# Two small numbers checked on VectorE instead of in every engine's registers, in an attention-and-mixer kernel on one core

## The chip, the core and the metric

The kernel runs on one core of a Trainium2 chip. A core has five engines that each work through a queue of their own: PE (TensorE, matmuls, with PEld for its weight loads), DVE (VectorE), ACT (ScalarE), POOL (GpSimd) and SP (SyncE, which here only issues DMAs). The metric is the device time of one execution in microseconds (us), lower is better.

## The reference, cut to what matters

Four sequences of 768 positions, 8 heads of 64 channels. Attention is banded: a query sees the first `n_global` keys (8 here) and the last `n_local` keys up to itself (96 here), with a linear distance bias. Its output goes through a token-mixing and a channel-mixing network.

```python
is_global = pos[None, :] < int(n_global)
is_local = (rel >= 0) & (rel < int(n_local))
keep = is_global | is_local
...
scores = scores - np.max(scores, axis=-1, keepdims=True)
a = np.exp(scores)
a = a / (np.sum(a, axis=-1, keepdims=True) + 1e-09)
return np.matmul(a, v).astype(np.float32)
...
h = np.maximum(xt @ w_tok1, 0.0) @ w_tok2
u = x + h.transpose(0, 2, 1)
h2 = np.maximum(u @ w_ch1, 0.0) @ w_ch2
return (u + h2).astype(np.float32)
```

## The kernel before

`n_global` and `n_local` are inputs, 64-bit integers that arrive as four 32-bit words `n`. The kernel holds two programs: `fast`, for `n_global` from 0 to 32 and `n_local` from 1 to 97, and `dense` for all else. Every engine reads the four words from DRAM into registers (first the pointer, `n_ptr`, then `n`), joins six comparisons in `near` with register instructions, and branches. The inputs here take `fast`.

`Early` is issued ahead of the branch. It starts the DMAs of the keys and queries of the first three units into ring slots `e0`, `e1` and `e3` (in the profile all are `e`, in order rows `e_58`, `e_59` and `e_61`; `e_60` is slot 2, a scratch area), the DMA of the two numbers into `ni` (all 128 partitions), and lets POOL prepare index patterns (`rel`, `far`, `glob`) and the table of powers `sc`. `warm` issues four dummy matmuls of 512 columns.

Behind the branch, `Fast.setup` scales query 0 on DVE (`scale`, result in `qs`), turns the numbers into three columns `few`, and builds the bias tiles `bo`, `bt` (DVE) and `be` (POOL) and the identity `ident` (POOL).

Then a planner (`Plan`) sets all further order. A work item has a rank, costs and dependences; `record` replays them in a model and issues them engine by engine. `InOrder` pins the order of one engine's instructions. The ranks come from a packed table `RANKS`, one number for each item. Items of a *unit* v (256 queries of a pair of heads; 48 units, 12 a batch): `load`, `q` (scale the query, mostly on POOL), `S` (scores `sp` on PE), `max` (DVE adds the bias and takes the maximum, into `pp` or `p`), `exp` (ACT), `sum`, `inv`, `norm`, transposes `tp` or DMA transposes by way of `r`, `V` (PE, into `op`), and `put` (into `x`, the attention's output; in batch 0 ACT copies the reciprocal factors, then DVE multiplies). Middle units (j = 1) span the border of two halves of `x`, so their `put` is two copies of 128 columns and two products. Weights come as 64-bit floats and are decoded by ACT and DVE (`w`, `t`). The mixers' matmuls are `pj`, `pu`, `hp` and `acc`; the last batch's channel mixer uses products `X`, `Y`, `W`, `ga` and `ge`.

## Time and profile before

| | |
|---|---|
| Median of three runs | 600.99 us (600.99 to 601.85) |
| The profiled execution: its time | 601.2 us |
| its span, first to last instruction | 599.1 us |
| PE, DVE, ACT, POOL busy | 587.3, 392.8, 297.3, 177.6 us |
| DMA | 64.22 MB, mean 107 GB/s |

The span is 2.1 us shorter than the execution's time; what lies outside it is not in the profile. Times in all views count from the span's start. Matmuls are pipelined and their ends are modelled, so PE's busy time overlaps and is no proof of a full rate; the distance from start to start tells more. A wait on several semaphores is put down to the one that came last by the profile. A `q` behind an engine's name stands for its sequencer, which loads registers, branches and issues DMAs.

### The profile page before, as it was taken

What the parts mean: (1) busy time and instruction counts of PE and PEld (TensorE: products, weight loads), DVE (VectorE), ACT (ScalarE), POOL (GpSimd) and SP (SyncE); (2) the same over time, 40 slices, a digit from 0 to 9 for tenths busy, and PEclk for the clock granted to TensorE, in tenths of its full rate; (3) what the DMA queues carried; (4) which work ended last, traced back from release to release, by engine and by line L of the source; (5) the groups of instructions that cost most, each with busy time, mean ns of one, the idle gap of its engine ahead of it and who ended that gap; (6) DMA issues with size and microseconds to landing.
All of it is one profiled execution on the core that took longest, in us unless ns stands there. A gap on an engine that the chain in (4) does not pass through costs nothing.

```text
span 599.1 us, 10678 instructions
## 1 busy us (share of the span) xinstructions
PE 587.3 (98%) x3804; PEld 537.7 (90%) x3804; DVE 392.8 (66%) x1026; ACT 297.3 (50%) x778; POOL 177.6 (30%) x265
## 2 busy tenths in 40 slices
PE   7999999999999999999999999999999999999996
PEld 4878898899899999999898999999889999999995
DVE  5999889999542475356666475555877569764323
ACT  5999988876521244255543135473543244232310
POOL 3345695664320054033242134243330020000000
PEclk9999999999999999999999999999999999999999
DMA  6981273576541014736736411657535001000003
GB/s 238 408 305 37 93 278 147 162 170 120 141 101 40 14 40 54 184 78 144 176 72 133 95 54 29 149 141 160 158 72 110 14 2 40 14 1 0 1 2 110
DMA packets 90717, 64.22 MB, mean 107 GB/s; under 512 B 76192, under 2 KB 80672, under 8 KB 90656
## 3 DMA queue, kind: packets, MB, share of 16 engines
q1 hardware_dynamic: 90512, 63.46, 39.4%
q8 instruction: 32, 0.52, 0.4%
q14 instruction: 29, 0.24, 0.1%
q10 hardware_dynamic: 144, 0.00, 0.0%
HBM read 38.80 MB, written 6.29 MB: 75 GB/s over the span
## 4 chain that ended last, share of the span: by engine, by line
PE 56%; DMA 3%; DVE 2%; issue 0%; ACT 0%; SPq 0%; DVEq 0%
PE acc L63 16%; PE hp L63 13%; PE ga L63 6%; PE X L63 4%; PE op L63 3%; PE pj L63 3%; PE pu L63 3%; PE ge L63 3%; PE sp L63 2%; PE W L63 2%; DMA p<-r 2%; PE Y L63 1%; DMA xn<-xr 1%; DVE r L63 1%; DVE o L63 1%; DVE p L63 0%
## 5 line engine op out<-in xcount | busy, mean ns | idle before, releaser
L63 PE MATMUL hp<-uh,wc 128*128 128x384 f32 x576 | 153.9, 336 | 0.2 <-DVE hl L63 0.2
L63 PE MATMUL acc<-hh,wc 128*128 128x384 f32 x576 | 149.0, 339 | 0.9 <-DVE st L63 0.9
L63 PEld LDWEIGHTS acc<-hh,wc 128*128 128x128 f32 x576 | 102.8, 188 | 7.4 <-issue 4.3
L63 PEld LDWEIGHTS hp<-uh,wc 128*128 128x128 f32 x576 | 104.6, 188 | 3.1 <-issue 1.7
L63 POOL TENSOR_SCALAR p<-p,st 128x256 f32<-128x256 f32 (+1 forms) x132 | 77.8, 607 | 78.1 <-ACT p L63 40.7
L63 PE MATMUL acc<-hl,wc 128*128 128x384 f32 x288 | 96.6, 335 | 0.1
L63 PE MATMUL hp<-ul,wc 128*128 128x384 f32 x288 | 96.3, 334 | 0.0
L63 DVE COPY r<-p 128x1024 uint16<-128x1024 uint16 (+1 forms) x89 | 63.7, 732 | 40.3 <-DMA p<-r 24.9
L63 ACT ACTIVATE hh<-hp 128x384 fp32r<-128x384 f32 x72 | 35.0, 488 | 83.2 <-PE hp L63 50.4
L63 ACT ACTIVATE p<-p,st 128x256 f32<-128x256 f32 (+1 forms) x132 | 63.5, 484 | 14.4 <-DVE st L63 13.8
L63 DVE SCALAR_TENSOR_TENSOR hl<-hp,hh 128x384 fp32r<-128x384 f32 x72 | 39.5, 551 | 33.6 <-ACT hh L63 32.0
L63 PEld LDWEIGHTS acc<-hl,wc 128*128 128x128 f32 x288 | 54.1, 188 | 0.4 <-DVE hl L63 0.4
L63 PEld LDWEIGHTS hp<-ul,wc 128*128 128x128 f32 x288 | 54.1, 188 | 0.2
L63 POOL TENSOR_TENSOR ul<-x,uh 128x384 fp32r<-128x384 f32 x23 | 25.4, 1109 | 94.3 <-ACT uh L63 92.4
L63 POOL TENSOR_SCALAR qs<-e,sc 128x256 f32<-128x256 f32 x36 | 22.7, 630 | 77.1 <-DMA e<-pk 59.1
L63 ACT COPY r<-p 128x1024 uint16<-128x1024 uint16 (+1 forms) x23 | 29.1, 1285 | 29.1 <-DMA p<-r 17.5
L63 PE MATMUL sp<-e,qs 64*128 64x256 f32 (+1 forms) x312 | 39.3, 389 | 3.0 <-DVE e L63 3.0
L63 PEld LDWEIGHTS sp<-e,qs 64*128 64x128 f32 x312 | 27.8, 197 | 10.9 <-issue 8.4
L63 ACT COPY x<-op 128x256 f32<-128x256 f32 (+1 forms) x64 | 18.9, 322 | 25.6 <-PE op L63 25.4
L63 PE MATMUL ga<-hh,wc 128*128 128x512 f32 x96 | 30.2, 395 | 0.0
L63 ACT ACTIVATE pp<-pp,st 128x256 f32<-128x256 f32 (+1 forms) x60 | 28.5, 483 | 1.9 <-DVE st L63 1.9
L63 DVE CUSTOM_DVE_ANT_0 p<-sp,be 128x256 f32<-128x256 f32 x48 | 20.0, 416 | 12.2 <-PE sp L63 10.8
(146 smaller groups left out, 1105.2 us busy)
## 6 DMA issues: line engine op xcount, KB each, us to landing
w<-wc SPq DMA_DIRECT2D x24, 512.0 KB, 5.4
e<-pk SPq DMA_DIRECT2D x24, 512.0 KB, 4.0
e<-pk SPq DMA_DIRECT2D x12, 384.0 KB, 3.9
out<-o SPq DMA_DIRECT2D x24, 192.0 KB, 1.9
unit<-pk SPq DMA_DIRECT2D x7, 512.0 KB, 8.7
w<-w SPq DMA_DIRECT2D x6, 512.0 KB, 9.5
out<-x SPq DMA_DIRECT2D x8, 192.0 KB, 2.1
p<-r SPq DMA_TRANSPOSE x56, 3.2
```

The costliest lines, as they stand in the source:

```text
L63: ins = getattr(self.engine, name)(*args, **kw)
```

## The change

The engines no longer load `n`. ACT's DMA brings the four words into one partition; DVE makes them floats (`num`), and tests all four ranges at once: (word - middle)² - (half width)² is at most 0 where a word is in range, and the maximum of the four is the `flag`. Every engine loads that one word from SBUF and branches on it. A matmul with a row of ones (`wide`) copies the numbers to all partitions. It stands between two groups of four dummy matmuls, where there was one group. The bias tiles `bo` and `bt` and the identity are built ahead of the branch. Queries are scaled in place, without `qs` and its three buffers and tokens; query 0 is scaled on ACT. `put` of middle units in batch 0 becomes one copy and one product of 256 columns. The planner starts from other busy times, and the table of ranks is new; of it only the first line of each is shown.

```diff
 FIRST = 0
-WARM = 4
+WARM = 4, 4
...
     def __getattr__(self, name):
         def call(*args, **kw):
             ins = getattr(self.engine, name)(*args, **kw)
-            if self.last is not None:
-                self.tc.add_manual_dep(ins.ins, self.last.ins.name, mybir.DependencyInfo(
-                    mybir.DependencyClass.NoSync, mybir.DependencyReason.DATA), reason="order")
-            self.last = ins
+            self.follow(ins)
             return ins
         return call
 
+    def follow(self, ins):
+        if self.last is not None:
+            self.tc.add_manual_dep(ins.ins, self.last.ins.name, mybir.DependencyInfo(
+                mybir.DependencyClass.NoSync, mybir.DependencyReason.DATA), reason="order")
+        self.last = ins
+
 
 class Early:
 
 
-    def __init__(self, tc, pool, pk, nb):
+    def __init__(self, ctx, tc, pool, pk, nb):
         nc = tc.nc
-        pe, dve, act, gps, sp = [InOrder(tc, e) for e in (nc.tensor, nc.vector, nc.scalar, nc.gpsimd, nc.sync)]
+        self.lines = pe, dve, act, gps, sp = [
+            InOrder(tc, e) for e in (nc.tensor, nc.vector, nc.scalar, nc.gpsimd, nc.sync)]
 
         self.slots = [pool.tile([P, 1024], F32, tag=f"e{i}", name=f"e{i}") for i in range(RING)]
-        self.ni = pool.tile([P, 4], I32, tag="ni", name="ni")
         self.ident = pool.tile([P, P], F32, tag="ident", name="ident")
         self.sc = pool.tile([P, H // 2], F32, tag="sc", name="sc")
-
+        self.bo, self.bt, self.be = [pool.tile([P, w], F32, tag=t, name=t) for t, w in (("bo", 256), ("bt", P), ("be", 256))]
+        bo = self.bo
+        ni = pool.tile([1, 4], I32, tag="ni", name="ni")
+        few = pool.tile([P, 32], F32, tag="first", name="first")
+        num, mid, far, n = few[0:1, 0:4], few[0:1, 4:8], few[0:1, 8:12], few[:, 20:23]
+        self.flag = few[0:1, 16:17]
+
+        act.dma_start(out=ni, in_=nb)
         t = self.slots[2]
-        self.zeros = t[:, 576:832].bitcast(BF16)
-        dve.memset(self.zeros, 0.0)
-
-        self.one = t[:, 832:836]
-        dve.memset(self.one, 0.0)
-        act.dma_start(out=self.ni, in_=nb.broadcast_to([P, 4]))
-        act.activation(out=self.one, in_=self.one, func=AF.Exp)
+        zeros, ones, one = t[:, 576:832].bitcast(BF16), t[0:1, 836:964], t[:, 832:836]
+        dve.memset(zeros, 0.0)
+        dve.memset(one, 0.0)
+        dve.memset(ones, 1.0)
+        for x, lo, hi in ((0, 0, 32), (1, 0, 0), (2, 1, 97), (3, 0, 0)):
+            gps.memset(mid[:, x:x + 1], (lo + hi) / 2)
+            gps.memset(far[:, x:x + 1], (hi - lo) ** 2 / 4)
+        act.activation(out=one, in_=one, func=AF.Exp)
         for i, x, k in ((0, 0, 128), (1, 1, 128), (2, 3, 0)):
             sp.dma_start(out=self.slots[x][:, k:640], in_=pk[i, :, k:640])
...
             gps.iota(t, pattern=[[step, t.shape[-1]]], base=base, channel_multiplier=mult,
                      allow_small_or_imprecise_dtypes=True)
 
-        self.rel, self.far, self.glob = t[:, 0:224], t[:, 224:448], t[:, 448:576]
-        iota(self.rel, 96, -1, 1)
-        iota(self.far, -768, 8, -8)
-        iota(self.glob, 0, 1, 0)
-        gps.affine_select(out=self.far, in_=self.far, compare_op=ALU.is_ge, fill=-TOP, base=96,
+        rel, other, glob = t[:, 0:224], t[:, 224:448], t[:, 448:576]
+        iota(glob, 0, 1, 0)
+        gps.tensor_scalar(out=glob, in0=glob, scalar1=-TOP, scalar2=-TOP / 2, op0=ALU.mult, op1=ALU.add)
+        iota(rel, 96, -1, 1)
+        iota(other, -768, 8, -8)
+        gps.affine_select(out=other, in_=other, compare_op=ALU.is_ge, fill=-TOP, base=96,
                           pattern=[[-1, 224]], channel_multiplier=1)
-        for x in (self.rel, self.glob):
-            gps.tensor_scalar(out=x, in0=x, scalar1=-TOP, scalar2=-TOP / 2, op0=ALU.mult, op1=ALU.add)
+        gps.tensor_scalar(out=rel, in0=rel, scalar1=-TOP, scalar2=-TOP / 2, op0=ALU.mult, op1=ALU.add)
         for i in range(H // 2):
             gps.memset(self.sc[:, i:i + 1], float(2 ** (2 * i + 1)))
         gps.tensor_scalar(out=self.sc[64:, :], in0=self.sc[64:, :], scalar1=2.0, scalar2=0.0, op0=ALU.mult, op1=ALU.add)
 
-    def warm(self, tc):
-        with tc.tile_pool(name="warm", bufs=1, space=PSUM) as ps:
-            wp = ps.tile([P, 512], F32, name="warm")
-            for i in range(WARM):
-                tc.nc.tensor.matmul(out=wp, lhsT=self.zeros[:, :P], rhs=self.zeros, start=i == 0, stop=i == WARM - 1)
+        space = ctx.enter_context(tc.tile_pool(name="warm", bufs=1, space=PSUM))
+        warm, wide = [space.tile([P, 512], F32, name=x) for x in ("warm", "wide")]
+        dve.tensor_copy(out=num, in_=ni)
+        for k, count in enumerate(WARM):
+            for i in range(count):
+                pe.matmul(out=warm, lhsT=zeros[:, :P], rhs=zeros, start=i == 0, stop=i == count - 1)
+            if k == 0:
+                pe.matmul(out=wide[:, :4], lhsT=ones, rhs=num, start=True, stop=True)
+
+        dve.tensor_tensor(out=num, in0=num, in1=mid, op=ALU.subtract)
+        dve.tensor_tensor(out=num, in0=num, in1=num, op=ALU.mult)
+        dve.tensor_tensor(out=num, in0=num, in1=far, op=ALU.subtract)
+        dve.tensor_reduce(out=self.flag, in_=num, op=ALU.max, axis=AX.X)
+
+        for i, x, m in ((0, 0, TOP), (2, 2, -8.0), (1, 2, TOP)):
+            dve.tensor_scalar(out=n[:, i:i + 1], in0=wide[:, x:x + 1], scalar1=m, scalar2=None, op0=ALU.mult)
+
+        dve.tensor_scalar(out=glob, in0=glob, scalar1=n[:, 0:1], scalar2=n[:, 2:3], op0=ALU.add, op1=ALU.min)
+        dve.scalar_tensor_tensor(out=bo[:, 32:], in0=rel, scalar=n[:, 1:2], in1=other, op0=ALU.add, op1=ALU.min)
+        dve.tensor_tensor(out=self.bt, in0=glob, in1=bo[:, 128:], op=ALU.max)
+        dve.tensor_copy(out=bo[:, :32], in_=glob[:, :32])
+        gps.memset(self.ident, 0.0)
+        gps.affine_select(out=self.ident, in_=self.ident, compare_op=ALU.not_equal, fill=1.0, base=0,
+                          pattern=[[-1, P]], channel_multiplier=1)
 
 
 class Plan:
...
-        events, now, count, form = [(t, 0, "free", None, None) for t in free.values()], 0.0, 0, None
-        held_port, marks, sharing, slow = 0.0, [], None, CRAWL
+        events, now, count, form = sorted((t, 0, "free", None, None) for t in free.values()), 0.0, 0, None
...
         nc = tc.nc
-        self.pe, self.dve, self.act, self.pool, self.sp = [
-            InOrder(tc, e) for e in (nc.tensor, nc.vector, nc.scalar, nc.gpsimd, nc.sync)]
+        self.pe, self.dve, self.act, self.pool, self.sp = early.lines
...
 
     def setup(self):
 
-        const, early, dve = self.const, self.early, self.dve
-        rel, far, glob = early.rel, early.far, early.glob
-        self.scale(0, dve)
-        n = self.few
-        for i, x, m in ((0, 0, TOP), (1, 2, TOP), (2, 2, -8.0)):
-            dve.tensor_scalar(out=n[:, i:i + 1], in0=early.ni[:, x:x + 1], scalar1=m, scalar2=None, op0=ALU.mult)
-
-        dve.tensor_scalar(out=glob, in0=glob, scalar1=n[:, 0:1], scalar2=n[:, 2:3], op0=ALU.add, op1=ALU.min)
-
-        self.bo, self.bt, self.be = [const.tile([P, w], F32, tag=t, name=t) for t, w in (("bo", 256), ("bt", P), ("be", 256))]
-        bo, be = self.bo, self.be
-        dve.scalar_tensor_tensor(out=bo[:, 32:], in0=rel, scalar=n[:, 1:2], in1=far, op0=ALU.add, op1=ALU.min)
-        dve.tensor_tensor(out=self.bt, in0=glob, in1=bo[:, 128:], op=ALU.max)
-        dve.tensor_copy(out=bo[:, :32], in_=glob[:, :32])
+        self.scale(0, self.act)
         for o, i, w in ((0, 32, 128), (160, 160, 96), (128, 0, 32)):
-            self.pool.tensor_scalar(out=be[:, o:o + w], in0=bo[:, i:i + w], scalar1=1.0, scalar2=0.0, op0=ALU.mult, op1=ALU.add)
-        self.pool.memset(self.ident, 0.0)
-        self.pool.affine_select(out=self.ident, in_=self.ident, compare_op=ALU.not_equal, fill=1.0, base=0,
-                                pattern=[[-1, P]], channel_multiplier=1)
+            self.pool.tensor_scalar(out=self.be[:, o:o + w], in0=self.bo[:, i:i + w], scalar1=1.0, scalar2=0.0, op0=ALU.mult, op1=ALU.add)
 
 
     def weights(self, n):
...
-        t["qs"] = qs = self.prep.tile([P, 256], F32, tag="qs", name="qs")
+        qs = t["q"]
...
-                    self.pe.matmul(out=g["sp"][e][:, o:o + w], lhsT=t["qs"][r, 128 * i:128 * i + 128],
+                    self.pe.matmul(out=g["sp"][e][:, o:o + w], lhsT=t["q"][r, 128 * i:128 * i + 128],
...
-                self.x[b, n, 0], self.x[b, n, 1] = x[:, :HC], x[:, HC:S]
+                self.x[b, n, 0], self.x[b, n, 1], self.x[b, n] = x[:, :HC], x[:, HC:S], x[:, 256:512]
...
+                if fold and j == 1:
+                    if m:
+                        continue
+                    x, w = self.x[b, n], 256
...
-                [f"load{v}"] if v > 2 else [], r - 8, ["q"])
+                [f"load{v}"] if v > 2 else [], r - 8)
-            [("sp", x, e) for x in twins for e in range(2)], ["q"], "rows")
+            [("sp", x, e) for x in twins for e in range(2)], (), "rows")
...
-            add(f"pi{v}", "act", 0.34 if j == 1 else 0.28, put, [f"V{v}"], r - 15)
-            add(f"put{v}", "dve", 0.45 if j == 1 else 0.35, lambda: put(1), [f"pi{v}"], r - 15, (), [("op", v)])
+            add(f"pi{v}", "act", 0.28, put, [f"V{v}"], r - 15)
+            add(f"put{v}", "dve", 0.35, lambda: put(1), [f"pi{v}"], r - 15, (), [("op", v)])
...
-IDLE, CRAWL = 2.0, 3.4
-
-BUSY = dict(dve=1.8, act=0.8, pool=3.0, sp=1.0)
+IDLE, CRAWL, COLD = 2.0, 3.4, 2.0
+
+BUSY = dict(dve=1.0, act=0.1, pool=1.0)
...
-    'c-jrnhkuL*0|4N=dvCt?-rkpadtYuOxA)HN<Sus^Qd^6*M(r)er<B+;=qF}HjiB1vq)62$wS}TaRge@x$oKu8|KK?VKL`^8#}U8wj0eQXW3U#~L{ulji'
...
+    'c-jqAcYKTo1HQZW?tSmQncJ5e$*tU;$*tsOZYDQ#D?6%YTe~P)1QAl=D^jZMXT=v36_gq=B5E`!Qma-&&9)RRN-OvI_xa~}e$QHzEy4)0W@OdCe9TzXP'
...
     nc = tc.nc
     nb = n.bitcast(I32).rearrange("(o a) -> o a", o=1)
     pool = ctx.enter_context(tc.tile_pool(name="early", bufs=1))
-    early = Early(tc, pool, pk, nb)
-    _, (g_lo, g_hi, l_lo, l_hi) = nc.values_load_multi_w_load_instructions(nb)
-    early.warm(tc)
-    near = (g_hi == 0) & (l_hi == 0) & (g_lo >= 0) & (g_lo <= 32) & (l_lo >= 1) & (l_lo <= 97)
-    with tc.If(near) as c:
+    with ExitStack() as start:
+        early = Early(start, tc, pool, pk, nb)
+        loads, (flag,) = nc.values_load_multi_w_load_instructions(early.flag.bitcast(I32))
+        for line in early.lines:
+            for i in loads:
+                if i.ins.engine == line.engine.engine:
+                    line.follow(i)
+    with tc.If(flag <= 0) as c:
         fast(tc, early, pk, nb, w1, w2, wc1, wc2, out)
     with c.Else():
         dense(tc, qT, kT, vn, nb, w1, w2, wc1, wc2, out)
```

Three places as the built programs have them. First PE, from behind its first four dummy matmuls to its first scores; before:

```order
L1366 TENSOR_LOAD n_ptr
L1366 TENSOR_LOAD n
L1369 REGISTER_ALU x11
L1369 COMPARE_AND_BRANCH
L63 MATMUL sp<-e_58,qs 128x128 [waits DMAHW1_49,DVE_49,PE_49]
...
L63 MATMUL sp<-e_58,qs 128x256 x2
L63 MATMUL sp<-e_59,qs 128x128 [waits DMAHW2_49,Activation_49]
...
L63 MATMUL sp<-e_59,qs 128x256 x2
L63 MATMUL sp<-e_61,qs 128x256 [waits DMAHW3_49,Activation_49]
```

and after:

```order
L63 MATMUL wide<-first,e_60 128x4 [waits DVE_49]
L63 LDWEIGHTS e_60
L63 MATMUL warm<-e_60 128x512
...
L1380 TENSOR_LOAD first [waits DVE_49]
L1385 COMPARE_AND_BRANCH
L63 MATMUL sp<-e_58 128x128 [waits DVE_49,DMAHW1_49,PE_49,Activation_49]
...
L63 MATMUL sp<-e_58 128x256 x2
L63 MATMUL sp<-e_61 128x256 [waits DMAHW3_49,Activation_49]
...
L63 MATMUL sp<-e_59 128x128 [waits DMAHW2_49]
```

The wide matmul and four more dummies (`warm`) stand ahead of one register load that waits for DVE; the eleven register instructions are gone, and the scores of slot 3 (unit 2) come ahead of those of slot 1 (unit 1). Next DVE, from behind its first two memsets to the first maxima (`ISA`); before:

```order
L1366 TENSOR_LOAD n_ptr
L1366 TENSOR_LOAD n
L1369 REGISTER_ALU x11
L1369 COMPARE_AND_BRANCH
L63 TENSOR_SCALAR qs<-e_58,sc 128x256 [waits DMAHW1_49,Pool_49]
L63 TENSOR_SCALAR few<-ni 128x1 [waits DMAHW0_49]
L63 TENSOR_SCALAR few<-ni 128x1 x2
L63 TENSOR_SCALAR e_60<-e_60,few 128x128 [waits DVE_49]
L63 SCALAR_TENSOR_TENSOR bo<-e_60,few 128x224
L63 TENSOR_TENSOR bt<-e_60,bo 128x128 [waits DVE_49]
L63 COPY bo<-e_60 128x32
L63 ISA pp,st<-sp,bt 128x128 [waits DVE_49,PE_49]
```

and after:

```order
L63 CAST first<-ni 1x4 [waits DMAHW0_49]
L63 TENSOR_TENSOR first<-first 1x4 [waits PE_49,Pool_49]
L63 TENSOR_TENSOR first<-first 1x4 [waits DVE_49]
L63 TENSOR_TENSOR first<-first 1x4 [waits DVE_49,Pool_49]
L63 TENSOR_REDUCE first<-first 1x1 [waits DVE_49]
L63 TENSOR_SCALAR first<-wide 128x1 x3
L63 TENSOR_SCALAR e_60<-e_60,first 128x128 [waits DVE_49,Pool_49]
L63 SCALAR_TENSOR_TENSOR bo<-e_60,first 128x224 [waits DVE_49,Pool_49]
L63 TENSOR_TENSOR bt<-e_60,bo 128x128 [waits DVE_49]
L63 COPY bo<-e_60 128x32
L1380 TENSOR_LOAD first [waits DVE_49]
L1385 COMPARE_AND_BRANCH
```

The conversion, three steps and a maximum are new (`first` holds numbers, flag and columns), and the bias moved ahead of the branch. Last ACT, from its branch to the first exponential (the row on `pp`); before:

```order
L1366 TENSOR_LOAD n_ptr
L1366 TENSOR_LOAD n
L1369 REGISTER_ALU x11
L1369 COMPARE_AND_BRANCH
L63 ACTIVATE qs<-e_59,sc 128x256 [waits DMAHW2_49,Pool_49]
L63 ACTIVATE qs<-e_61,sc 128x256 [waits DMAHW3_49]
L63 ACTIVATE pp,st<-pp,st 128x128 [waits DVE_49]
```

and after:

```order
L1380 TENSOR_LOAD first [waits DVE_49]
L1385 COMPARE_AND_BRANCH
L63 ACTIVATE e_58<-e_58,sc 128x256 [waits DMAHW1_49,Pool_49]
L63 ACTIVATE e_59<-e_59,sc 128x256 [waits DMAHW2_49]
L63 ACTIVATE e_61<-e_61,sc 128x256 [waits DMAHW3_49]
L63 ACTIVATE pp,st<-pp,st 128x128 [waits DVE_49]
```

ACT has three scalings ahead of its first exponential where it had two, and they write the slots themselves.

## Rows read from the trace of the kernel before

**Rows 1.** The page, part 1: busy us, share of the span, number of instructions.

```profile
PE 587.3 (98%) x3804; PEld 537.7 (90%) x3804; DVE 392.8 (66%) x1026; ACT 297.3 (50%) x778; POOL 177.6 (30%) x265
```

**Rows 2.** Windows: stretch and its length, busy us by engine (number), clock, DMA share, GB/s.

```profile
6.10:10.70 4.60, 4.60 (x25) 3.63 (x25) 2.96 (x19) 3.12 (x13) 1.86 (x7) 1.00 0.77 212
10.70:20.00 9.30, 9.25 (x86) 7.43 (x85) 9.11 (x39) 8.81 (x35) 2.15 (x5) 1.00 1.02 404
20.00:40.00 20.00, 19.16 (x199) 15.08 (x199) 19.11 (x67) 18.99 (x60) 9.13 (x11) 1.00 1.01 395
40.00:70.00 30.00, 30.00 (x283) 25.45 (x279) 27.43 (x103) 28.74 (x93) 18.54 (x30) 1.00 0.14 44
...
150.00:450.00 300.00, 298.94 (x1881) 276.59 (x1880) 175.60 (x478) 127.72 (x341) 88.57 (x144) 1.00 0.44 102
```

**Rows 3.** PE's waits: us in total, times, longest.

```profile
PE sp L63 <- DVE e L63: 3.0, 1, 3.0
...
PE acc L63 <- DVE st L63: 0.9, 2, 0.5
PE tp L63 <- DVE pp L63: 0.8, 1, 0.8
```

**Rows 4.** Timeline of DVE, start: start, length, operation, shape, number [idle before, releaser].

```profile
4.90 0.35 DVE L63 TENSOR_SCALAR qs<-e,sc 128x256 f32<-128x256 f32 x1 [3.75 <-DMA e<-pk]
5.17 0.27 DVE L63 TENSOR_SCALAR few<-ni 128x1 f32<-128x1 int32 x3
5.48 0.35 DVE L63 TENSOR_SCALAR e<-e,few 128x128 f32<-128x128 f32 x1
...
6.43 0.27 DVE L63 COPY bo<-e 128x32 f32<-128x32 f32 x1
```

**Rows 5.** Timeline of PE, start.

```profile
1.20 1.89 PE L115 MATMUL warm<-e 128*128 128x512 bf16 x4 [1.20 <-DVE e L63]
6.10 4.64 PE L63 MATMUL sp<-e,qs 64*128 64x128 f32 x24 [3.02 <-DVE e L63]
```

**Rows 6.** Register loads, by source line: duration in ns min/median/max, first and last start.

```profile
L1366 DVEq TENSOR_LOAD <-n_ptr x1: 919/919/919, 0.8 to 0.8; - x1
L1366 PEldq TENSOR_LOAD <-n_ptr x1: 1287/1287/1287, 1.2 to 1.2; - x1
...
L1366 PEldq TENSOR_LOAD <-n x1: 2075/2075/2075, 2.5 to 2.5; - x1
...
L1366 POOLq TENSOR_LOAD <-n x1: 633/633/633, 4.2 to 4.2; - x1
```

**Rows 7.** The line of the branch, PE's rows, same columns (591.4 is the end).

```profile
L1369 PEldq ALU_OP  x11: 33/43/43, 4.7 to 5.7; - x11
...
L1369 PEldq COMPARE_BRANCH  x2: 90/1695/3300, 5.8 to 591.4; - x2
```

**Rows 8.** DMA issues: number, KB each, median us from issue to landing.

```profile
out<-o SPq DMA_DIRECT2D x24, 192.0 KB, 1.9
...
ni<-n ACTq DMA_DIRECT2D x1, 2.0 KB, 3.7
```

**Rows 9.** Timeline of PE around 13.7 us.

```profile
13.74 1.13 PE L63 MATMUL sp<-unit,qs 64*128 64x256 f32 x8
```

**Rows 10.** Groups of ACT to 75 us, by shape: busy us, mean ns, idle before.

```profile
L63 ACT COPY x<-op 128x256 f32<-128x256 f32 x11 | 4.2, 385 | 0.5 <-PE op L63 0.5
...
L63 ACT COPY x<-op 128x128 f32<-128x128 f32 x8 | 1.7, 264 | 0.7 <-PE op L63 0.6
...
L63 ACT ACTIVATE qs<-e,sc 128x256 f32<-128x256 f32 x2 | 1.0, 508 | 3.0 <-DMA e<-pk 3.0
```

**Rows 11.** Timeline of ACT, 7 to 16 us, its two pieces with idle time.

```profile
8.09 0.40 ACT L63 ACTIVATE pp<-pp,st 128x128 f32<-128x128 f32 x1 [1.38 <-DVE st L63]
...
11.32 0.51 ACT L63 ACTIVATE pp<-pp,st 128x256 f32<-128x256 f32 x1 [0.49 <-DVE st L63]
```

**Rows 12.** Timeline of SP, first issue behind its branch.

```profile
5.71 0.33 SPq L63 DMA_DIRECT2D unit<-pk  x1
```

More of the change, by code (lines that the diff above doesn't have):

```diff
@@ L159, in after @@
             return w["end"] + (self.LATENCY[w["engine"]] if w["lag"] is None else w["lag"])
-        events, now, count, form = [(t, 0, "free", None, None) for t in free.values()], 0.0, 0, None
-        held_port, marks, sharing, slow = 0.0, [], None, CRAWL
+        events, now, count, form = sorted((t, 0, "free", None, None) for t in free.values()), 0.0, 0, None
+        held_port, marks, sharing, slow = 0.0, [], None, COLD
         while events:
@@ L269, in __init__ @@
         self.pool_of = pool
-        const = self.const = pool("const", 1)
         self.ring = early.slots
@@ L278, in __init__ @@
         self.tok = pool("tok", 1, **left)
-        self.prep = pool("prep", 3, **left)
         self.soft = pool("soft", 8, **left)
@@ L286, in __init__ @@
         self.early = early
-        self.ident, self.sc = early.ident, early.sc
+        self.ident, self.sc, self.bo, self.bt, self.be = early.ident, early.sc, early.bo, early.bt, early.be
         self.t, self.x, self.u = {}, {}, {}
@@ L1175 @@
+    '6ZVubKSm%mf8o^`pg$K`Sru<?^oZeJ6`|I8^uE#M#PdCd&X9?c<{`sO*OO9_tLi$vny{@dTTaTZmuk^YD-5G`)fF{Q*puIy$Mu&P*PK8sZXRUGM&||*x'
+    '%L1suv`&4U^O7YGm~v)NRWkYoA7G@zwDM>3elK^_0r0gu8}X^Lu7x1ynPvCMWTKXf!(l'
 )
```

83 lines of the change are left out of this document (40 added, 43 removed).

## The prediction

> **What bounds the kernel now.** I read the busy line of the page first: the reader is to see PE at 98% of a 599.1 us span, with DVE at 66% and ACT at 50% [rows 1]. An early shift of PE's work can therefore reach the end, unless a later stage holds it back. The windows by stage come next [rows 2]. From 10.7 to 70 us ACT and DVE are nearly full beside it: 8.81 and 9.11 of 9.30 us, 18.99 and 19.11 of 20, 28.74 and 27.43 of 30. That is the attention of batch 0 together with the decoding of the weights, and there ACT and DVE set the pace. From 150 to 450 us PE is busy 298.94 of 300 us and the two are far from full: there PE leads.
>
> The list of PE's own waits [rows 3] has one large entry, the 3.0 us ahead of the first scores, put down to DVE; the next are 0.9 and 0.8 us. The change works at the place of the first. The label deserves doubt: the query that the first scores read was scaled at 4.90 for 0.35 us [rows 4], so DVE had released them by about 5.3. Yet they began at 6.10 [rows 5]; before that PE had done nothing but 1.89 us of dummy matmuls. The register loads show what was later [rows 6]: PE loads a pointer at 1.2 for 1.29 us and the four words at 2.5 for 2.08 us, eleven register instructions follow from 4.7 to 5.7, and its branch stands at 5.8 and takes 0.09 us [rows 7]. So PE's own branch ended last before 6.10, not DVE's scaling.
>
> **The change part by part.** First the removed work. Each engine loses the pointer load, the four-word load and eleven register instructions. On PE that is 2.5 to 5.8 plus the pointer: all of the time from 1.2 to 5.9.
>
> In its place stands a chain through several engines. I follow it with durations of rows, and where there is none, with bounds.
>
> *Landing of the two numbers.* They are loaded by a DMA issued at 0.74, now into one partition. In 128 partitions it took 3.7 us to land; the quickest group of transfers, the 192 KB stores, needs 1.9 us [rows 8]. One small packet is nearer to the quick end, since it has not 128 descriptors to work off. I take 2.2 us, so 2.94; the bounds are 2.64 and 4.44.
>
> *DVE's conversion and PE's broadcast.* The conversion of an int32 column takes about 0.15 us, read from three that took 0.27 together with starts 0.07 apart [rows 4]; with a little for the semaphore, 3.14. The new matmul stands behind four dummies that end at 3.09 [rows 5], so it does not wait for them. An f32 matmul of four columns is not in the trace. The nearest rows are eight f32 score records in 1.13 us, 0.14 each [rows 9], and the four dummies in 1.89, 0.47 each [rows 5]; with a lone matmul's result on the way I take 0.42, near the upper end. Result at 3.6. The first range instruction overwrites the operand in place, so it waits for that matmul.
>
> *Three range instructions and the maximum on DVE.* Each depends on the one before. The three columns in a row are done at about 5.44, and the next instruction, which needs them, starts at 5.48 [rows 4]: 0.15 plus 0.04 makes about 0.18 us a step. Four steps, 0.72: the word is there at 4.35. Bounds 0.4 and 1.0.
>
> *The one word, read by five engines from SBUF.* Nothing in the trace reads SBUF into a register. Four words from DRAM took 0.63 us on POOL, which came last, and 2.08 on PE, which ran beside others [rows 6]. All ten loads, five pointers of two words and five times four words, fill the time from 0.83 to about 4.81, 0.13 us for each of 30 words if they pass one at a time. Five words then take 0.66 us. I take that; the bounds are 0.16, a quarter of POOL's, and 2.08. Word in the register: 5.0.
>
> The Trainium skill, "Runtime: NRT & Kernel Launch", section "Instruction fetch mechanics", prices such a load at about 200 ns per register. The rows agree on POOL, 0.16 us per word, and not on PE, 0.52. By that figure the word would be there at 4.55 and the gain of the start would be 0.75 us instead of 0.3, an estimate that the sum below does not use.
>
> *Branch, scaling, first scores.* A branch costs 0.09 us on PE and some 0.15 until the next instruction. ACT scales query 0 from about 5.2; the query has landed by then, since DVE scaled it at 4.90. A scaling on ACT takes 0.51 us [rows 10] where DVE needed 0.35. So the first scores start at 5.8 instead of 6.10. **Term 1: -0.3 us**, with bounds of -0.8 (load 0.16) and +1.2 (landing at 4.44, or a load of 2.08).
>
> *What the start is worth.* The first exponential starts at 8.09 and ACT then runs on, but for 0.49 us at 11.32 where the maxima of the third unit came late [rows 11]. Both belong to slow matmuls: the 24 records of the first three score groups took 4.64 us [rows 5], 0.19 us each though half of those of two groups are narrow, where eight wide ones later took 1.13, 0.14 each [rows 9]. The windows print a granted clock of 1.00 for that stretch too [rows 2], but the spacing is that of the lower level, 1.2 GHz, after 3.0 us of idleness. The eight dummies now reach to about 4.95, so PE idles for 0.9 us ahead of the first scores, not 3.0. If the clock is up by then, group 0 takes about 0.8 us less and the 0.49 us goes too; if not, the gap shrinks only by what the earlier start gives. I take half of the 0.8 and most of the 0.49: **term 2: -0.8 us**, bounds 0 and -1.3. The bias is built ahead of the branch, from 4.4 to 6.0, since the seven instructions from the three columns on took 1.53 us [rows 4], beside the loads and the scaling. It is hidden, since the first maximum needs scores that end at 6.6 at the earliest; without that cover it would cost its old 1.5 us. ACT's two further scalings end by 6.6, also ahead of its first exponential. POOL gets eight tiny memsets and the identity ahead of its branch; the memsets come first in its queue, and the identity is not used before the transposes, after the first exponentials.
>
> *Scaling in place and the merged copies.* The scaling stays the same instruction with another target. It costs nothing: POOL, which does nearly all, is idle most of the time. For the middle units of batch 0 eight copies of 128 columns on ACT become four of 256: 1.7 us busy become four times 0.385, or 1.5 [rows 10]. ACT sets the pace there. **Term 3: -0.2 us** (0 to -0.4).
>
> *The new ranks.* They move nearly every row behind the first dozen. The order rows show group 2 ahead of group 1 and three scalings on ACT; the work itself is the same. What order can win back is bounded by PE's listed waits behind the first, 0.9 + 0.8 = 1.7 us [rows 3]. What it can lose is open; two more such entries cost about 2. **Term 4: -0.3 us**, bounds -1.7 and +2.
>
> Sum: -0.3 - 0.8 - 0.2 - 0.3 = -1.6 us. The profiled execution took 601.2 us, 2.1 more than its span, so 599.6; the median of the runs shown lies 0.2 below it. **Predicted: 599.4 us.**
>
> **Rivals.** *It does not reach the end.* DMA has a share of 1.01 to 1.02 from 10.7 to 40 us [rows 2]; if the loads of units and weights, not ACT, set that stage, the earlier start only makes ACT wait for the transfers. They start when SP has passed its branch, which would be 5.2 instead of 5.71 [rows 12], so only these 0.5 us are left of all terms: 600.5. For it: the full DMA rows. Against: ACT and DVE are as full.
> *It wins more.* The clock is up before the first scores and the new order removes the listed waits: terms of 0.8 + 1.3 + 0.4 + 1.5 make 4.0, so 597.0. For it: DVE and ACT have less to do in the stage they bound.
> *The word comes late (slower).* Place: the five register loads behind DVE's maximum. All five engines now stand at one semaphore, and everything behind them, SP's transfers too, is late with them. If the numbers land as slowly as before (4.44) and the load takes PE's 2.08, the word is there at 7.9 and the scores start at 8.7, 2.6 us late; terms 3 and 4 give 0.5 back: 603.1. It decides for slower by 0.2% from a word at about 7.0 on; either of the two alone gives 601.6 to 601.7, no change.
> *The new order loses (slower).* PE stands at a fixed place for a result of the DMA transposes in batches 2 and 3, and DVE's queue holds it: +2 there against -1.3 of terms 1 to 3 would be 601.7, and twice as much 603.7; it decides from a loss of 2.5 on. For it: all rows move. Against: PE's waits behind the start were 1.7 us in all with the old ranks.
>
> **How the numbers follow.** 0.2% is 1.2 us, about what a measurement of this kernel can tell from no change. Forecast (598.2 to 600.3) 0.50; does not reach the end (600 to 601.5) 0.24; wins more (596 to 598.2) 0.11; word late 0.06; order loses 0.09. Faster than 599.8 are four fifths of the forecast, all of "wins more" and little of the rest: 0.53. Slower than 602.2 are the last two and 0.02 for what I have not thought of: 0.17. The same is left with 0.30. The range of 596.8 to 602.2 leaves out the two slow cases and a third of "wins more", about 2 in 10.
>
> **What will show it.** Right or wrong step by step: the landing of the numbers (2.9), the word's register loads on all engines (start 4.35, done 5.0), PE's first score (5.8) and its spacing, ACT's first exponential (7.0 to 7.4 instead of 8.09) with no idle piece before 16 us, PE's list of waits without a 3.0 entry, and ACT busy 10.7 to 70. If a load takes 2 us, or new entries of a microsecond stand in PE's waits, the prediction is wrong at terms 1 or 4.

## The result, and the profile after

After: 609.69 us (median of four runs, 608.51 to 610.65) against 601.42 for the kernel before on the same chip: 1.0136 times as long (95% interval 1.0115 to 1.0157). The prediction was 599.4, faster; the kernel became 8.3 us slower. The profiled execution took 610.65 us, its span 608.8.

The page, part 1, as [rows 1]:

```profile
PE 592.3 (97%) x3810; PEld 537.7 (88%) x3810; DVE 398.8 (66%) x1029; ACT 294.8 (48%) x776; POOL 171.0 (28%) x270
```

DVE has 6 us more work than before. Two groups grow: the tiny additions told below take 10.4 us in all against 7.0, and the new order gives DVE ten products `ul` where it had five (first before, then after); POOL has 18 of them in place of 23.

```profile
L63 DVE TENSOR_TENSOR ul<-x,uh 128x384 fp32r<-128x384 f32 x5 | 3.4, 680 | 0.3
```

```profile
L63 DVE TENSOR_TENSOR ul<-x,uh 128x384 fp32r<-128x384 f32 x10 | 7.4, 745 | 2.9 <-ACT uh L63 2.5
```

What these five cost is not known: no run moves them back alone. PE's waits, as [rows 3]:

```profile
PE acc L63 <- ACT hh L63: 1.5, 1, 1.5
PE warm L63 <- DVE e L63: 1.2, 1, 1.2
PE sp L63 <- POOL e L63: 1.1, 2, 0.7
PE op L63 <- ACT r L63: 1.1, 1, 1.1
PE tp L63 <- DVE x L63: 0.9, 1, 0.9
PE acc L63 <- DVE p L63: 0.8, 1, 0.8
PE acc L63 <- DVE hl L63: 0.6, 1, 0.6
```

The 3.0 us ahead of the first scores are gone, as forecast. In their place stand six new, shorter entries all over the program (`warm` stood there before too). The windows by stage, as [rows 2], with two new stretches:

```profile
10.70:20.00 9.30, 8.84 (x92) 6.87 (x91) 8.29 (x34) 9.30 (x35) 1.66 (x5) 1.00 1.02 402
20.00:40.00 20.00, 18.89 (x188) 14.31 (x184) 18.79 (x70) 17.99 (x56) 8.20 (x12) 1.00 0.97 365
40.00:70.00 30.00, 30.00 (x277) 25.60 (x272) 28.72 (x97) 29.09 (x91) 17.86 (x29) 1.00 0.11 34
70.00:80.00 10.00, 9.35 (x68) 7.40 (x67) 8.07 (x13) 5.90 (x14) 5.65 (x6) 1.00 0.90 298
90.00:100.00 10.00, 8.38 (x49) 7.47 (x48) 9.93 (x26) 8.30 (x20) 7.40 (x10) 1.00 0.18 72
```

The two new stretches in the kernel before:

```profile
70.00:80.00 10.00, 10.00 (x76) 8.63 (x74) 8.91 (x19) 8.29 (x19) 6.37 (x6) 1.00 0.75 262
90.00:100.00 10.00, 10.00 (x72) 9.03 (x71) 8.75 (x16) 7.98 (x16) 5.63 (x6) 1.00 0.18 71
```

From 70 to 80 us ACT is now busy only 5.90 of 10 us, 8.29 before, and DMA is at 0.90, 0.75 before; from 90 to 100 DVE is full and PE is not.

**The start went as predicted up to the first score.** The timeline of all engines to 9.5 us:

```profile
1.95 0.19 DVE L63 CAST first<-ni 1x4 f32<-1x4 int32 x1 [0.67 <-DMA ni<-n]
...
3.01 0.58 PE L63 MATMUL wide<-first,e 1*128 1x4 f32 x2
...
4.33 0.14 DVE L63 TENSOR_REDUCE first<-first 1x1 f32<-1x4 f32 x1
...
5.76 3.23 PE L63 MATMUL sp<-e 64*128 64x128 f32 x24 [0.34 <-DVE bt L63]
...
7.88 0.40 ACT L63 ACTIVATE pp<-pp,st 128x128 f32<-128x128 f32 x1 [1.38 <-DVE st L63]
```

and the register loads of PE and DVE, by source line (ns min/median/max, first and last start), as [rows 6]:

```profile
L1380 PEldq TENSOR_LOAD <-first x1: 490/490/490, 4.5 to 4.5; - x1
L1380 DVEq TENSOR_LOAD <-first x1: 546/546/546, 5.5 to 5.5; - x1
```

The numbers landed by 1.95 (forecast 2.94), but the broadcast stood behind the four dummies until 3.01, so nothing came of it. The word was there at 4.47 (4.35), in PE's register at 5.0 (5.0), the first score came at 5.76 (5.8). The first exponential came at 7.88 instead of 8.09; forecast were 7.0 to 7.4.

One trace of the old start is a thin base for this. There are four, and the kernel before has the latest start of them: the first score at 6.10, in the runs below at 5.88 (e3_place), 5.83 (e2_order) and 5.74 (e16_before_xw); the first exponential at 8.09, 7.87, 7.82 and 7.73. The earliest:

```profile
5.74 4.36 PE L63 MATMUL sp<-e,qs 64*128 64x128 f32 x24 [2.65 <-DVE few L63]
...
7.73 0.40 ACT L63 ACTIVATE pp<-pp,st 128x128 f32<-128x128 f32 x1 [1.55 <-DVE st L63]
```

The new start has its first score at 5.75 or 5.76 in all fourteen profiles, and the first exponential at 7.81 to 7.88 in eleven of them, at 7.16 in three. So the gain at the first score lies between nothing and 0.34 us, and at the exponential most executions show none.

**Where the time went.** I took PE's matmuls of each trace in order, gave each the usual spacing of its kind, and read at what time the same amount of work had been done. The differences to the kernel before, in us (the last four columns are runs told below):

```
time in before   after   e1_front   e2_order   e8_w14   e13_four
     26.0        -1.3     -0.9       -0.9      -0.7      -0.7
     31.5        -0.1     -0.9       +0.4      +0.5      +0.5
     76.8        +1.9     -1.0       +2.6      +1.3      +1.9
     97.2        +4.5     -1.0       +3.7      +2.9      +1.8
    139.8        +6.6     -1.0       +5.6      +4.8      +2.0
    306.7        +6.2     -1.4       +4.6      +3.5      +1.1
    327.3        +8.6     -1.4       +8.6      +5.1      +1.4
    592.3        +8.4     +0.2       +8.5      +5.0      +1.5
```

The changed kernel is 1.3 us ahead at 26 us, against this one trace of the kernel before, and that is gone by 31.5. The loss comes in pieces: 66 to 77, 77 to 97, 130 to 140, and at 318 us. My theory from here: the new order alone loses the time, at a few places where an engine's queue stands in order for something late. The rivals: the new start or the scaling in place costs it.

### The profile page after: what moved, and what is told of

Same layout as the page of the kernel before. It is cut to its first block, busy times and chain, and to the rows that moved or that the text cites. A ratio compares the mean times of both kernels' runs of the same rounds, so it can differ in the third digit from the quotient of the medians.

```text
span 608.8 us, 10686 instructions
## 1 busy us (share of the span) xinstructions
PE 592.3 (97%) x3810; PEld 537.7 (88%) x3810; DVE 398.8 (66%) x1029; ACT 294.8 (48%) x776; POOL 171.0 (28%) x270
## 4 chain that ended last, share of the span: by engine, by line
PE 55%; DMA 5%; DVE 2%; POOL 1%; issue 1%; ACT 1%; SPq 0%; DVEq 0%; POOLq 0%; ACTq 0%
PE hp L63 14%; PE acc L63 13%; PE ga L63 5%; PE X L63 4%; PE pu L63 4%; DMA p<-r 3%; PE pj L63 3%; PE op L63 3%; PE ge L63 3%; PE sp L63 2%; PE W L63 2%; DMA e<-pk 1%; PE Y L63 1%; DVE r L63 1%; POOL p L63 1%
## 5 line engine op out<-in xcount | busy, mean ns | idle before, releaser
L63 DVE COPY r<-p 128x1024 uint16<-128x1024 uint16 (+1 forms) x93 | 66.5, 735 | 49.0 <-DMA p<-r 23.4
L63 POOL TENSOR_SCALAR e<-e,sc 128x256 f32<-128x256 f32 x36 | 20.2, 564 | 95.3 <-DMA e<-pk 92.0
L63 ACT COPY r<-p 128x1024 uint16<-128x1024 uint16 (+1 forms) x19 | 24.8, 1312 | 32.3 <-DMA p<-r 25.9
L63 PE MATMUL sp<-e 64*128 64x256 f32 (+1 forms) x312 | 37.7, 379 | 1.5 <-POOL e L63 1.1
L63 POOL TENSOR_TENSOR ul<-x,uh 128x384 fp32r<-128x384 f32 x18 | 19.7, 1101 | 63.2 <-ACT uh L63 63.0
L63 PEld LDWEIGHTS sp<-e 64*128 64x128 f32 x312 | 26.6, 191 | 9.6 <-issue 2.9
L63 PE MATMUL op<-r,e 128*64 128x128 f32 (+1 forms) x304 | 26.7, 317 | 1.1 <-ACT r L63 1.1
L63 DVE CUSTOM_DVE_ANT_0 p<-sp,bo 128x256 f32<-128x256 f32 x66 | 27.6, 418 | 0.0
```

Of the source, the lines that this page charges most:

```text
L63: ins = getattr(self.engine, name)(*args, **kw)
```

## The experiments

Ratios are to the kernel before on the same chip, with their 95% interval.

**First series: which part.** e1_front is the whole change with the ranks and planner numbers of before (the changed kernel is `-`; lines of the table and of the planner's model are left out):

```diff
-        held_port, marks, sharing, slow = 0.0, [], None, COLD
+        held_port, marks, sharing, slow = 0.0, [], None, CRAWL
...
-                [f"load{v}"] if v > 2 else [], r - 8)
+                [f"load{v}"] if v > 2 else [], r - 8, ["q"])
...
-            add(f"pi{v}", "act", 0.28, put, [f"V{v}"], r - 15)
-            add(f"put{v}", "dve", 0.35, lambda: put(1), [f"pi{v}"], r - 15, (), [("op", v)])
+            add(f"pi{v}", "act", 0.34 if j == 1 else 0.28, put, [f"V{v}"], r - 15)
+            add(f"put{v}", "dve", 0.45 if j == 1 else 0.35, lambda: put(1), [f"pi{v}"], r - 15, (), [("op", v)])
...
-BUSY = dict(dve=1.0, act=0.1, pool=1.0)
+BUSY = dict(dve=1.8, act=0.8, pool=3.0, sp=1.0)
...
-    'c-jqAcYKTo1HQZW?tSmQncJ5e$*tU;$*tsOZYDQ#D?6%YTe~P)1QAl=D^jZMXT=v36_gq=B5E`!Qma-&&9)RRN-OvI_xa~}e$QHzEy4)0W@OdCe9TzXP'
+    'c-jrnhkuL*0|4N=dvCt?-rkpadtYuOxA)HN<Sus^Qd^6*M(r)er<B+;=qF}HjiB1vq)62$wS}TaRge@x$oKu8|KK?VKL`^8#}U8wj0eQXW3U#~L{ulji'
...
```

> The whole change but for the order: the new start, scaling in place and merged copies, with the ranks and planner numbers of before. If the new order alone loses the time (theory), PE keeps the 1.3 us that its work was ahead between 13 and 25 us of the changed kernel's trace: 600.1 us against 601.4 for the kernel before, and no delay of PE's work grows between 66 and 146 us. If the start is lost again by itself and the scaling in place (each unit's buffer is held until the scaled query has been read) slows the loads (rival 1), it stays near 609. If DMA bounds the stage to 70 us (rival 2), the lead is gone by 31 us: 601.4.

Measured: 601.41 us, 0.9993 (0.9982 to 1.0004), not the 600.1 expected. e2_order is the reverse, the old start with the new order; queries are scaled in place and the copies merged in it too:

> The start of before (four words into registers on each engine, bias and branch as before, query 0 scaled on DVE), with scaling in place, merged copies, and the new ranks and planner numbers. If the new order alone loses the time (theory), it loses 9.7 us here and has no lead of 1.3 to set against it: 610 to 611.5 us. If the loss comes from the new start meeting the order (rival 1: transfers and POOL's work fall at other times), it is nearer to the kernel before, 601 to 604.

Measured: 609.67 us, 1.0145 (1.0127 to 1.0163). e3_place is the kernel before with these two edits alone:

```diff
-        t["qs"] = qs = self.prep.tile([P, 256], F32, tag="qs", name="qs")
+        qs = t["q"]
...
+                if fold and j == 1:
+                    if m:
+                        continue
+                    x, w = self.x[b, n], 256
```

> The kernel before with two parts of the change alone: queries scaled in place and four merged copies in place of eight. If neither costs anything (theory): 601.2 us, 0.2 less than the kernel before, no change that can be measured. If scaling in place holds buffers or the merged copies come late (rival 1): 603 to 609, with new waits of PE on transfers of units.

Measured: 601.95 us, 1.0003 (0.9992 to 1.0013). So the order alone loses the time, and both rivals fall. In its trace the start of e1_front keeps a lead of 1 us up to 375 us and loses it between 400 and 475; at the end no gain can be measured. That trace is one of the three with the first exponential at 7.16, and it is set against the latest start of the old kind, so most executions have less to lose.

**Second series: the places.** On ACT, the rows from 76 to 82 us of the changed kernel:

```profile
76.64 0.35 ACT L63 COPY x<-op 128x256 f32<-128x256 f32 x1
80.33 0.68 ACT L63 ACTIVATE w<-w 128x512 int32<-128x512 uint8 x1 [3.34 <-DMA w<-wc]
```

ACT stands 3.34 us for one weight piece. Before, its only wait of this kind from 70 to 150 us was this one:

```profile
ACT w L63 <- DMA w<-wc: 0.5, 1, 0.5
```

SP's queue, before (first) and after (second), shows how the loads stand there:

```profile
33.15 14.55 SPq L63 DMA_DIRECT2D w<-wc  x4
69.49 3.37 SPq L63 DMA_DIRECT2D e<-pk  x3
72.95 0.86 SPq L63 DMA_DIRECT2D w<-wc  x2
80.23 0.33 SPq L63 DMA_DIRECT2D e<-pk  x1
```

```profile
68.95 0.33 SPq L63 DMA_DIRECT2D e<-pk  x1
69.33 1.16 SPq L63 DMA_DIRECT2D w<-wc  x1
71.98 0.94 SPq L63 DMA_DIRECT2D e<-pk  x2
72.97 0.90 SPq L63 DMA_DIRECT2D w<-wc  x2
76.57 0.33 SPq L63 DMA_DIRECT2D e<-pk  x1
77.00 11.18 SPq L63 DMA_DIRECT2D w<-wc  x8
```

Before, piece 13 goes out by 48 us, ahead of unit 16. After, it stands behind unit 16, for whose buffer SP waits until 68.95, and five more loads start by 73.45, within 4.5 us. Piece 14, the fourth of these, lands 7.3 us after its issue (80.31); before it took 5.4 (78.35). The second place is a pair of transposes at 132 us with a unit's load between them, the third four transposes at 305 us behind two units' loads. The next four kernels move issues of SP and nothing else. After the planner has made its order, a list takes a first item behind a second:

```diff
+BEHIND = (('load16', 'w13'),)
...
+        for x, y in BEHIND:
+            self.order.remove(x)
+            self.order.insert(self.order.index(y) + 1, x)
```

That is e4_weight. e5_inject puts `('w13', 'load16')` into e1_front; e6_turns has `('load21', 'turn201'), ('xt202', 'turn321'), ('xt203', 'xt202')`; e7_all has e4's and e6's.

> The changed kernel with one issue moved: the load of weight piece 13 goes ahead of the load of unit 16 on SP's queue, as it stands before the change. Theory (a blocked transfer piles loads up): behind unit 16, which SP holds until 68.95, five loads start within 4.5 us, piece 14 lands at 80.31 and ACT stands 3.3 us for it; with piece 13 issued by 48 us, piece 14 lands at about 78.4 as before the change, and 2 to 3 us of the loss between 66 and 100 us go: 606.7 to 607.7 us. Rival (DVE's and ACT's own order in that stage loses the time): no change, 609.7.

> The opposite: the new start with the old order (601.4 us), and in it alone piece 13 put behind unit 16. Theory: ACT comes to stand for piece 14, and 2 to 3 us are lost between 70 and 100 us: 603.4 to 604.4 us. Rival (the old order has the slack to take it, or the place does not matter): 601.4.

> The changed kernel with the two later places mended alone: the load of unit 21 goes behind the second of two DMA transposes that it stood between (its neighbour landed 5.1 us after its issue, where the same transposes took 3.3 before the change), and of four transposes behind the loads of units 34 and 35 the two of the mixer go behind those of the attention. Theory (a unit load in front makes transposes late, and PE stands for what they turn): 1.5 us come back at 141 us and 1 to 1.5 at 318: 606.7 to 607.2. Rival (these stalls only take up slack that is lost anyway): 609.7.

> Both mends together, four issues of SP moved and nothing else. Theory: their gains add, 4.5 to 5.5 us: 604.2 to 605.2, three fifths of what the new order lost. Rival (only the first matters): 607. Rival (neither): 609.7.

Measured: e4_weight 607.69 us, 1.0101 (1.0083 to 1.0118); e5_inject 605.96, 1.0065 (1.0042 to 1.0087); e6_turns 610.14, 1.0146 (1.0129 to 1.0164); e7_all 609.14, 1.0137 (1.0116 to 1.0158). One issue put elsewhere costs the good order 0.9993 to 1.0065, 4.3 us, more than the 2 to 3 expected. The waits of e5_inject, ACT's from 60 to 100 us and PE's: ACT stands for piece 13 itself, and PE for what ACT then makes late.

```profile
ACT w L63 <- DMA w<-wc: 3.6, 1, 3.6
```

```profile
PE pu L63 <- ACT ph L63: 2.9, 1, 2.9
```

The stall has a second price, which stands in no list of waits. Behind it the granted clock is 0.50, the lower of the two levels (1.2 GHz), from 74.5 to 81.4 us:

```profile
76.00:78.00 2.00, 2.00 (x8) 1.92 (x7) 1.46 (x4) 0.95 (x2) 0.63 (x1) 0.50 0.98 395
```

At half the rate PE loses about 3.4 us in these 6.9 (an estimate). The profiled execution is the slowest of the six, 608.68 us with a mean clock of 0.992; the fastest, 603.24, has 0.998. So the 4.3 us are a stall and a fall of the clock, and to judge by these mean clocks the fall does not come in every execution.

In e4_weight the size came out as expected and the reason did not: piece 14 still landed at 79.85, 6.9 us after its issue, and ACT stood 4.0 us for it (below); what went was the wait of 1.1 us for piece 13 and what hung on it. In e6_turns the trace has about 1 us back at 140 us and 1.1 lost again at 318: DVE's next split there began at 311.33, when the first of the moved transposes had landed (311.21) and given its buffer back. So the expectation of e7_all fell too. By this one trace, moving those two was wrong.

**Third series: two causes in one stage.** From 85 to 117 us DVE is the fullest engine, 30.52 of 32 us (28.14 before). Its group of tiny additions (1e-9 to the sums of the exponentials) in the changed kernel, and the same row of e1_front:

```profile
L63 DVE TENSOR_SCALAR st<-st 128x4 f32<-128x4 f32 x4 | 3.9, 966 | 0.0
```

```profile
L63 DVE TENSOR_SCALAR st<-st 128x4 f32<-128x4 f32 x2 | 0.3, 155 | 0.0
```

The mean of the four is 966 ns in the one order; three of them take 1.18 to 1.27 us. In the other order it is 155 ns. DVE's timeline at 89 us, with POOL's beside it:

```profile
89.49 1.18 DVE L63 TENSOR_SCALAR st<-st 128x4 f32<-128x4 f32 x1
90.70 0.18 DVE L63 RECIPROCAL st<-st 128x4 f32<-128x4 f32 x1
```

```profile
89.35 1.30 POOL L63 TENSOR_TENSOR wc<-t,wc 128x512 fp32r<-128x512 f32 x1 [2.11 <-ACT wc L63]
```

The addition ends at 90.67, just as POOL's instruction does (90.65); the other two long ones end 0.03 us behind such a POOL product as well (97.00 and 96.97, 117.73 and 117.70). The time is counted as busy, so no list of waits shows it; four times 966 less 155 ns are 3.2 of DVE's 6 us more. The Trainium skill, "SBUF — State Buffer", section "SBUF: two separate sides", says that VectorE and GpSimd share one pair of ports under an exclusive lock: a VectorE instruction in a two-port mode, or one that reads two inputs from SBUF beside a GpSimd instruction that reads there, is blocked until a GpSimd instruction that started first has ended. The three ends agree with such a wait, but no row tells whether the addition ran in such a mode, ten other additions took 0.15 to 0.22 us beside an open POOL instruction of another kind, and no run here moves the POOL instruction alone. e8_w14 has `('load16', 'w13'), ('load18', 'w14'), ('load19', 'load18')`; e9_sums leaves the additions out, and the reciprocals read the sums themselves; e10_both has both and `('load21', 'turn201')`; e11_front_sums is e1_front without additions.

```diff
-            engine.tensor_scalar(out=st[:, 8:12], in0=st[:, 4:8], scalar1=EPS, scalar2=0.0, op0=ALU.add, op1=ALU.add)
+            pass
...
-            dve.reciprocal(out=g["st"][:, 8:12], in_=g["st"][:, 8:12])
+            dve.reciprocal(out=g["st"][:, 8:12], in_=g["st"][:, 4:8])
```

> The changed kernel with weight piece 14 brought in earlier: on SP's queue piece 13 goes ahead of unit 16 as in the last series, and piece 14 ahead of units 18 and 19. In the last series piece 14 still landed at 79.85, 6.9 us after its issue, and ACT stood 4.0 us for it. Theory (that one wait is the loss of the stage to 85 us): issued at 69.4, it lands by 75, the wait of 4.0 us goes, and 2.5 to 3.5 us come back against the changed kernel: 606.2 to 607.2. Rival (DVE sets the pace of that stage, and ACT's wait only lies in front of it): 607.7, as with piece 13 alone.

> The changed kernel without the 48 instructions that add 1e-9 to the sums of the exponentials, which are at least 1; the reciprocals read the sums themselves, all else stands where it stood. Theory: four of these tiny additions on DVE take 0.81 to 1.27 us where the others take 0.19, because each stands until an instruction of POOL that started before it ends (89.35 and 1.30 long, the addition from 89.49 to 90.67), and DVE sets the pace between 85 and 116 us; 3.5 us come back there: 605.7 to 606.5. Rival (DVE makes up for them while PE has other work): 609 to 609.7.

> The changed kernel with all that these series point to: pieces 13 and 14 earlier, the load of unit 21 behind the second transpose, and no additions. Theory: the gains add, 3 + 3.5 + 1.5 of the 9.7 us that the new order lost: 601.5 to 603. Rival (they overlap, since each only delays the same DVE queue): 604.5 to 606.

> The new start with the old order (601.4 us in the first series), without the same additions. In the old order none of them takes over 0.51 us. Theory: nothing is lost at such a place there, so only their plain length can be gained where DVE sets the pace, 0 to 1.5 us: 600 to 601.4. Rival (an addition waits for POOL wherever it stands): 598 to 599.5, as much as in the new order.

Measured: e8_w14 607.39 us, 1.0103 (1.0085 to 1.0122); e9_sums 608.75, 1.0117 (1.0096 to 1.0138); e10_both 604.31, 1.0044 (1.0028 to 1.0060); e11_front_sums 601.81, 1.0002 (0.9991 to 1.0013). ACT's wait for the piece, 60 to 100 us, in e4_weight and in e8_w14:

```profile
ACT w L63 <- DMA w<-wc: 4.0, 1, 4.0
```

```profile
ACT w L63 <- DMA w<-wc: 1.8, 1, 1.8
```

The two are not the same wait. In e8_w14 piece 14 landed in time, at 75.32, and ACT stands 1.8 us for the next piece instead, at 81.18 behind its landing at 81.16. The time stays: piece 14 alone buys nothing beyond piece 13. Without the additions PE is 2.6 us ahead of the changed kernel at 140 us and only 0.5 at the end: e9_sums alone is not told apart from the changed kernel. Most of its lead goes between 307 and 340 us, and part of that is the clock again. In e9_sums and e10_both PE stalls 1.8 and 1.7 us at 316 and 312 us, and then the granted clock is 0.50 for 3.4 us, here in e10_both:

```profile
316.00:318.00 2.00, 2.00 (x17) 1.43 (x14) 1.13 (x3) 0.56 (x2) 1.81 (x4) 0.50 0.04 12
```

The 24 products `op` in that stretch take 3.24 us (e9_sums) and 3.63 (e10_both); in the changed kernel, with a stall of 1.5 us there and a clock of 1.00, they take 1.96. e10_both, 1.0136 to 1.0044, has 5.5 us back. The two alone give 2.0 and 1.1, and the load of unit 21 about 1; with the intervals of these runs their sum is not told apart from 5.5. In the old order the additions cost nothing that can be measured.

**Fourth series: the rest.** The changed kernel at 318 us, PE, and ACT's rows ahead of it:

```profile
319.95 0.62 PE L63 MATMUL acc<-hh,wc 128*128 128x384 f32 x2 [1.48 <-ACT hh L63]
```

```profile
316.21 0.19 ACT L63 ACTIVATION_READ_ACCUMULATOR p<-p,st 128x1 f32 x1
318.22 1.34 ACT L63 COPY r<-p 128x1024 uint16<-128x1024 uint16 x1 [1.82 <-DMA p<-r]
319.43 0.47 ACT L63 ACTIVATE hh<-hp 128x384 fp32r<-128x384 f32 x1
```

ACT stands for a transpose, joins it, and only then does the ReLU that PE waits for. e12_relu has `('join331', 'fh41')` alone, e13_four that and all of e10_both; e14_front_xw is e1_front with `('xw30', 'max461')`.

> The changed kernel with one instruction of ACT moved: at 318 us the copy that joins a transposed half goes behind the ReLU of channel step 41. Theory: F41's product was ready at 316.4, but ACT stood for a transpose that landed at 318.14 and copied until 319.5, so the ReLU came at 319.43 and PE stood 1.48 us; with the ReLU in front PE goes on and 1.4 to 1.7 us come back: 608 to 608.3. Rival (the values that need the join are the next on PE and stall by as much): 609.7.

> The changed kernel with all mends: pieces 13 and 14 earlier, unit 21 behind the transpose, no additions, and that ReLU ahead of the join. Theory: the stall at 312 us, 1.85 long there, goes on top of what the others gave: 602.5 to 603, within 1.5 us of the old order with the new start. Rival (the loss moves on to the next transpose): 604.3.

> The new start with the old order, and one DVE copy moved: the join of a transposed tile of batch 3 goes behind the maxima of unit 46. In the old order with the new start DVE stands 2.3 us for that tile at 428 us, the attention behind it is late, and PE stands twice for a bank at 440, 1.2 us in all. Theory: those 1.2 us and the lead of the start that they swallowed come back: 600.0 to 600.4, faster than the kernel before by 0.2 to 0.3%. Rival (the bank comes late for another reason too, or the tile is late for the mixer): 601.4 or more.

Measured: e12_relu 608.21 us, 1.0105 (1.0088 to 1.0122); e13_four 602.74, 1.0020 (1.0006 to 1.0034); e14_front_xw 600.50, 0.9975 (0.9966 to 0.9984). ACT in e12_relu, the ReLU now in front:

```profile
315.85 0.49 ACT L63 ACTIVATE hh<-hp 128x384 fp32r<-128x384 f32 x1
317.77 1.36 ACT L63 COPY r<-p 128x1024 uint16<-128x1024 uint16 x1 [1.43 <-POOL p L63]
```

e12_relu and e13_four came out as the theory said, e14_front_xw 0.1 us above its 600.0 to 600.4. The traces of the first two have neither the stall near 316 us nor a fall of the clock there. In e14_front_xw one DVE copy stands elsewhere; DVE in e1_front before and after the move:

```profile
430.58 1.04 DVE L63 COPY xw<-xn 128x1024 uint16<-128x1024 uint16 x1 [2.32 <-DMA xn<-xr]
```

```profile
440.35 0.75 DVE L63 COPY xw<-xn 128x1024 uint16<-128x1024 uint16 x1 [0.71 <-ACT r L63]
```

**Fifth series.** e15_inputs is the changed kernel with the old table of ranks alone; e16_before_xw is the kernel before with `('xw30', 'max461')`.

> The changed kernel with the old table of ranks alone: new start, new planner numbers. If the new table itself makes the loss: 600.5 to 603, about the old order with the new start (601.4). If the planner's new numbers make it, whatever the table: 607 to 610.

> The kernel before with the one DVE copy of batch 3 moved, as in the version that came out at 600.5. If the move alone gains (two stalls of PE, 0.9 us in all there): 600.8 to 601.2. If the old start swallows it: 601.5 to 602; then the new start is worth its 1 us only together with it.

Measured: e15_inputs 666.64 us, 1.1078 (1.1060 to 1.1096), which neither expectation held; e16_before_xw 600.15, 0.9974 (0.9964 to 0.9983), a little better than expected. The old table with the new numbers makes a third order, with waits of PE up to 9.2 us; its mean granted clock is 0.965, with 0.50 in most of the stretch from 509 to 567 us, so part of its loss is the clock. The new table with the old numbers was not run, so these runs don't tell which of the two spoils the new pair. And the gain of the moved copy needs no new start.

## Why the prediction was wrong

- **Term 4, the new ranks, failed.** It stood at -0.3 with a bound of +2, "two more such entries". Measured, the order alone makes the time 1.0145 times as long, 8 to 9 us (e2_order), while the start with the old order gives 0.9993 (e1_front) and the scaling in place 1.0003 (e3_place). The bound was drawn from PE's waits with the old ranks; these say what the old order had left, not what another one makes; the prediction itself called the loss open. The edit that moved nearly every row got the smallest thought and no wide end.
- **"The new order loses"** named the sign, with a chance of 0.09, and too little (601.7 to 603.7). It put the place at transposes in batches 2 and 3. One place is of that kind (318 us, e12_relu: a wait of 1.5 us). The others are a weight load behind a unit's load on SP, DVE additions beside POOL, and a load between two transposes. Together, with the ReLU, they are 1.0136 to 1.0020, 7 of the 8.3 us (e13_four). By themselves only the weight load (e4_weight) and the ReLU (e12_relu) are just clear of the noise; the additions and the load between the transposes are not, and that they hold their part is read from the traces. Of the rest, 1.2 us go between 26 and 31 us, where nothing was tried, and the five `ul` that went to DVE stay there in e13_four too.
- **Term 1 had the chain right and its gain is not shown**: word 5.0, first score 5.76, -0.34 of the forecast -0.3 against the one trace that it was worked out from. The other three traces of the old start have 5.74 to 5.88, so that agreement is in part luck. The landing was 1 us better than taken, and the dummies ahead of the broadcast hid it.
- **Term 2 was too hopeful for most runs**: 7.88 in this trace is -0.2, not -0.8, and no gain over the 7.73 to 7.87 of the other three traces of the old start. Of the fourteen profiles with this start three have 7.16.
- **Term 3 was not seen**: with scaling in place and merged copies alone 1.0003 (0.9992 to 1.0013). The loss of up to 0.8 us or gain of 0.5 that the interval leaves cannot be told.
- **"It does not reach the end"** was right for the three terms, at another place: the start with the old order gives 0.9993, and its lead goes not in the DMA-full stage but at 400 to 475 us. With the copy moved both starts come out the same, 0.9975 and 0.9974, so the new start is worth nothing that these runs can show, even without that stall.
- The 1.7 us that I bounded as an order's gain were real in one place: e16_before_xw took 1.5 us with one move.

The best version is the kernel before with one copy moved (e16_before_xw, 600.15), or the same with the new start (600.50): both faster than both kernels.

## What to carry to other kernels

A table that sets the whole order is the largest edit in a diff even where it looks like data: price it by running the order alone, and give it the widest range. In queues that run in order, look for instructions that stand for a transfer in front of work that is ready; one moved issue or copy was worth 1.5 to 4.3 us here, the 4.3 with a fall of the clock in it, and a mend at one place may show little until the next place is mended too. Look at PE's granted clock behind each of its stalls, for the fall can cost as much as the stall. Before a start is called faster, look at several traces of the old one. An engine that is full may be holding instructions that themselves wait: compare the mean length of the same group in two traces, since such a wait stands in no list of waits.
